# Turning v for a channel-attention kernel: eight TensorE transposes per group, or block loads and one VectorE transpose

## The chip, the cores and the metric

The kernel runs on one core of a Trainium2 chip. The metric is the device time of one execution in microseconds (us). The engines are called by the names that the profile uses: PE is TensorE (matmul; PEld is its weight load), DVE is VectorE, ACT is ScalarE, POOL is GpSimd, and SP is the engine that issues the DMAs here.

## What is computed

For each of four batches, q, k and v are 6080 tokens by 256 channels, all float32. Channel attention is followed by a feed-forward layer with a rational activation:

```
qn = q / (norm(q, axis=tokens) + 1e-6);  kn likewise
a  = softmax(kn.T @ qn / tau)            # 256 x 256, per batch
x  = v @ a                               # tokens x 256
h  = x @ w_in                            # 256 -> 2048
P  = a0 + a1 h + a2 h^2 + a3 h^3
Q  = 1 + |b0| |h| + |b1| h^2
out = (P / (Q + 1e-6)) @ w_out           # 2048 -> 256
```

## The kernel before

The attention matrix of a batch is folded into w_in once per batch (`fuse`), so that the main work on the tokens is h = v @ (a @ w_in), the activation, and the product with w_out. The tokens of a batch are cut into 12 groups, 11 of 512 tokens (four rows of 128) and one of 448; over four batches that is 48 groups. The 2048 hidden units are cut into eight pairs of 128, so a group has eight calls of `pair`. Each pair computes h in two PSUM banks (`mm1`, 12 matmuls of 512 columns: high and low parts of the weights and of v, the low times low product left out), runs the activation in about ten steps on ACT, DVE and POOL, and accumulates the product with w_out in PSUM (`mm2`, two halves, each with its own step). `finish` copies the group's result out and stores it.

The matmul `mm1` wants v with channels on the partitions. `values` makes that: it loads the group's v with tokens on the partitions (tile `vst`, one buffer), turns it with eight PE transposes of 128x128 into a PSUM buffer of the kind `hx`, and splits it there into a high part `vhi` (ACT, a copy that rounds) and a low part `vlo` (DVE, the difference). There are two buffers each of `vhi` and `vlo`, three of `hx` (which the pairs use for h) and one accumulator `acc`; together they fill PSUM.

The order of the instructions on each engine is not the order of the program text. Every step is handed to a `Planner` with an engine, a cost, a due time ("key") and the buffers that it reads and writes. The planner plays the engines forward in time: an engine that is free takes the ready step with the lowest key whose buffers are free. What it writes out is the order on each engine, and nothing else; costs, keys and latencies have no other effect on the chip. Buffers of the kinds in its `fifo` list are given out in the order of the keys. The due times come from the tables `LAG` (steps of a pair) and `TIME` (all else). Steps marked as using the port (all of POOL's, and DVE's steps that read and write only SBUF) are played one after the other between DVE and POOL.

Batch 0's scores are computed before the first group; 12 halves of batch 1's keys and queries are also read and multiplied early (`FRONT`); the rest of the next batch's attention is mixed into the groups. Each half of a group's q and k is loaded by two DMAs, squared on ACT and summed on POOL (some of batch 0's on DVE). The weights w_in and w_out arrive as 64-bit floats and are converted on DVE; four pieces of w_out are converted late, in the tiles `cv` and `cv2`.

Of the kernel before, what the change touches and what calls it, by code (L numbers as in the profile page):

```python
# [18 lines left out]


LAG = {
    "first": 2.42, "prod": 2.04, "abs": -4.64, "line": 9.56, "second": 3.75, "sum": -23.6, "slope": 5.71,
    "num1": 23.17, "num2": 21.53, "root": 8.83, "one": -1.7, "square": -3.23, "again": 5.54, "quot": 8.31,
    "last": 10.3, "out": 23.21,
}
TIME = {
    "pair": 3.57, "start": 48.71, "load": 1.9, "softmax": 48.77, "in": 5, "late_in": 3.83, "out0": 2.3,
    "out": 5.39, "attn0_0": -0.02, "attn_0": 0.98, "attn0": 3.82, "attn": 2.42, "attn1": 91.81, "value": 3.3,
    "fuse": 1.77, "finish": 10.12, "front": 45.32, "front_pace": 2.4,
}  # L30


# [35 lines left out]
class Planner:  # L68
# [42 lines left out]
    def order(self):  # L111
# [10 lines left out]
        busy["SP"] = 3.0  # L122
        events, out, now = [(3.0, 2, 0, None)], [], 0.0
        port = {"DVE": 0.0, "POOL": 0.0}
        for s in self.steps:
            if not s.need:
                heapq.heappush(ready[s.eng], (s.key, s.n, s))
# [12 lines left out]
        while left:  # L140
            for e in ready:
                while busy[e] <= now and ready[e]:
                    skipped, pick = [], None
                    while ready[e]:
                        entry = heapq.heappop(ready[e])
                        if fits(entry[2]):
                            pick = entry[2]
                            break
                        skipped.append(entry)
                    for entry in skipped:  # L150
                        heapq.heappush(ready[e], entry)
# [15 lines left out]
                    heapq.heappush(events, (busy[e], 0, pick.n, pick))  # L167
                    heapq.heappush(events, (busy[e] + self.HOP[e], 1, pick.n, pick))
            if not left:
                break  # L170
            assert events, [(e, h[0][0], [b.tag for b in h[0][2].new], dict(free)) for e, h in ready.items() if h]
            now = events[0][0]
            while events and events[0][0] <= now:
                _, what, _, s = heapq.heappop(events)
                if what == 2:
                    continue
                for t in s.after:
                    if (what == 0) == (t.eng == s.eng and s.eng != "SP"):
# [13 lines left out]
def tile_channel_attention_rational_ffn(  # L192
# [15 lines left out]
    P = 128  # L208
# [387 lines left out]


    def pair(m, at, vparts, w, acc):
# [20 lines left out]
                        )  # L619
                    idx += 1  # L620

        step("PE", 2.8 * s, at, mm1, [whi, wlo, vhi, vlo], [hx])

        if m >= NFP and p in FACTORED:
            fn = lambda: act.activation(c(kk), c(hx), AF.Abs, scale=b1)
            step("ACT", 1.12 * s, at + LAG["first"], fn, [hx], [kk])
            fn = lambda: dve.scalar_tensor_tensor(c(d), c(kk), b0, c(hx), op0=ALU.add, op1=ALU.mult)
            step("DVE", 1.28 * s, at + LAG["prod"], fn, [kk, hx], [d])
            fn = lambda: act.activation(c(d), c(d), AF.Abs)
            step("ACT", 1.02 * s, at + LAG["abs"], fn, [d], [d])  # L630
        else:
            fn = lambda: act.activation(c(d), c(hx), AF.Square)
            step("ACT", 1.02 * s, at + LAG["first"], fn, [hx], [d])
            fn = lambda: pool.tensor_scalar(c(d), c(d), b1, ONE, op0=ALU.mult, op1=ALU.add)
            step("POOL", 1.13 * s, at + LAG["line"], fn, [d], [d])
            fn = lambda: act.activation(c(kk), c(hx), AF.Abs, scale=b0)
            step("ACT", 1.12 * s, at + LAG["second"], fn, [hx], [kk])
            fn = lambda: pool.tensor_tensor(c(d), c(d), c(kk), op=ALU.add)
            step("POOL", 2.38 * s, at + LAG["sum"], fn, [d, kk], [d])

        fn = lambda: act.activation(c(y), c(hx), AF.Identity, scale=a3, bias=a2)
        step("ACT", 1.2 * s, at + LAG["slope"], fn, [hx], [y])
        fn = lambda: dve.tensor_tensor(c(y), c(y), c(hx), op=ALU.mult)
        step("DVE", 1.22 * s, at + LAG["num1"], fn, [y, hx], [y])
        fn = lambda: dve.scalar_tensor_tensor(c(hx), c(y), a1, c(hx), op0=ALU.add, op1=ALU.mult)
        step("DVE", 1.28 * s, at + LAG["num2"], fn, [y, hx], [hx])
# [3 lines left out]
        step("ACT", 1.06 * s, at + LAG["root"], fn, [d], [r])  # L650
        if m >= NFP and p in FACTORED:
            fn = lambda: pool.tensor_scalar(c(d), c(d), ones[:, 0:1], ONE, op0=ALU.mult, op1=ALU.add)
            step("POOL", 1.13 * s, at + LAG["one"], fn, [d], [d])
        fn = lambda: act.activation(c(r), c(r), AF.Square)
        step("ACT", 1.06 * s, at + LAG["square"], fn, [r], [r])
        fn = lambda: pool.tensor_tensor(c(d), c(d), c(r), op=ALU.mult)
        step("POOL", 2.38 * s, at + LAG["again"], fn, [d, r], [d])
        fn = lambda: dve.scalar_tensor_tensor(c(hx), c(hx), a0, c(r), op0=ALU.add, op1=ALU.mult)
        step("DVE", 1.28 * s, at + LAG["quot"], fn, [hx, r], [hx])
# [3 lines left out]
        step("DVE", 1.28 * s, at + LAG["last"], fn, [d, hx], [g])  # L663

        def mm2(i):
            for t in range(T):
# [5 lines left out]

        for i in range(2):
            old = [] if p == 0 and i == 0 else [acc]
            step("PE", 1.72, at + LAG["out"] + 0.1 * i, lambda i=i: mm2(i), [g, w_out_ok[p], *old], [acc])

    def finish(G, at, acc):
        b, g = divmod(G, NG)
        base, pn = groups[g]
        orow = buf("orow", [P, T, C])  # L680
        step("ACT", 1.05, at, lambda: act.copy(orow[:pn], acc[:pn]), [acc], [orow])
# [64 lines left out]
```

## Time and profile before

| what | value |
|---|---|
| time, median of 3 runs | 2692.95 us (2692.72 to 2694.38) |
| span of the profiled execution | 2694.6 us, 32473 instructions |
| PE busy | 2653.3 us, 98% |
| DVE, ACT, POOL busy | 2247.6, 2195.5, 2106.4 us (83%, 81%, 78%) |
| granted TensorE clock, mean | 0.995 |

The span runs from the first to the last instruction of the program with its last DMA; no other time is listed for the profiled execution. A busy time is the share of the span in which an engine had an instruction in flight. The ends of matmuls are modelled, so the start of one matmul to the start of the next tells more than their durations.

### The profile page before, as it was taken

The page shows a single profiled execution, that of the slowest core. Times are in us where ns is not written, and L with a number is a line of the kernel's source. Part 1 is how long each engine was busy: PE and PEld are TensorE (multiplying, and loading weights), DVE is VectorE, ACT ScalarE, POOL GpSimd, SP SyncE. Part 2 cuts the span into 40 slices and gives each one's busy share as a digit, 9 for nine tenths or more (in the row PEclk, how much of TensorE's full clock was granted, in tenths as well). Part 3 has the DMA queues.
Part 4 walks back from the last instruction along what each step waited for, and adds up shares of the span by engine and source line. Part 5 has one row for each costly group of instructions (what it writes and reads, how often), then busy time and mean ns, then how long its engine had stood idle before and what let it go on. Part 6 is the DMA issues. An engine that isn't in the chain of part 4 may idle for free.

```text
span 2694.6 us, 32473 instructions
## 1 busy us (share of the span) xinstructions
PE 2653.3 (98%) x12200; PEld 2271.6 (84%) x12200; DVE 2247.6 (83%) x1987; ACT 2195.5 (81%) x2227; POOL 2106.4 (78%) x1104
## 2 busy tenths in 40 slices
PE   7999999999999999999999999999999999999999
PEld 6778888888888888888888888888888888888887
DVE  7988888888878778788888878788888888888886
ACT  5778888888788888788878888877887888888885
POOL 6789877877678788877868888877875787787785
PEclk9999999999999999999999999999999999999999
DMA  9402000000011111100001111100000000000000
GB/s 325 134 32 80 28 16 32 16 18 30 16 31 47 55 55 48 45 32 31 17 16 31 55 55 48 47 30 32 15 16 16 31 16 16 32 16 17 31 9 15
DMA packets 69325, 110.10 MB, mean 41 GB/s; under 512 B 5296, under 2 KB 53936, under 8 KB 69168
## 3 DMA queue, kind: packets, MB, share of 16 engines
q1 hardware_dynamic: 69168, 108.03, 12.3%
q8 instruction: 96, 1.57, 0.2%
q14 instruction: 61, 0.50, 0.1%
HBM read 83.10 MB, written 24.90 MB: 40 GB/s over the span
## 4 chain that ended last, share of the span: by engine, by line
PE 90%; DVE 3%; POOL 1%; issue 1%; ACT 1%; DVEq 0%; POOLq 0%
PE acc L43 47%; PE hx L43 44%; DVE hx L43 1%; POOL d L43 1%; DVE g L43 1%; DVE sq L43 0%; ACT r L43 0%; DVE cv L43 0%; DVE uu L43 0%; DVE y L43 0%; DVE n L43 0%; DVE vlo L43 0%; DVE e L43 0%; ACT d L43 0%; DVE sm L43 0%
## 5 line engine op out<-in xcount | busy, mean ns | idle before, releaser
L43 PE MATMUL acc<-w_out_sb,g 128*128 128x256 f32 (+1 forms) x6144 | 1371.1, 379 | 0.0
L43 PEld LDWEIGHTS acc<-w_out_sb,g 128*128 128x128 f32 (+1 forms) x6144 | 1157.0, 189 | 167.6
L43 POOL TENSOR_TENSOR d<-d,r 128x1024 f32<-128x1024 f32 (+1 forms) x384 | 906.2, 2362 | 187.1 <-ACT r L43 172.9
L43 PE MATMUL hx<-vhi,w 128*128 128x512 f32 (+1 forms) x3072 | 892.5, 401 | 10.4 <-DVE g L43 5.5
L43 PEld LDWEIGHTS hx<-vhi,w 128*128 128x128 f32 x3072 | 579.1, 189 | 125.5 <-ACT sq L43 10.3
L43 DVE TENSOR_TENSOR uu<-uu,hx 128x1024 f32<-128x1024 f32 (+1 forms) x384 | 462.4, 1204 | 189.0 <-ACT uu L43 187.9
L43 POOL TENSOR_TENSOR d<-d,uu 128x1024 f32<-128x1024 f32 (+1 forms) x243 | 573.9, 2362 | 20.3
L43 DVE SCALAR_TENSOR_TENSOR hx<-hx,coef,r 128x1024 f32<-128x1024 f32 (+1 forms) x384 | 490.3, 1279 | 118.1 <-ACT r L43 101.2
L43 DVE SCALAR_TENSOR_TENSOR g<-d,hx 128x1024 f32<-128x1024 f32 (+1 forms) x384 | 463.5, 1207 | 47.2 <-POOL d L43 11.1
L43 DVE SCALAR_TENSOR_TENSOR hx<-uu,coef,hx 128x1024 f32<-128x1024 f32 (+1 forms) x384 | 489.6, 1275 | 7.8
L43 PE MATMUL hx<-vlo,w 128*128 128x512 f32 (+1 forms) x1536 | 474.3, 390 | 0.0
L43 ACT ACTIVATE uu<-hx,coef 128x1024 f32<-128x1024 f32 (+1 forms) x384 | 458.6, 1194 | 0.0
L43 ACT ACTIVATE uu<-hx,babs 128x1024 f32<-128x1024 f32 (+1 forms) x384 | 424.4, 1105 | 26.6 <-PE hx L43 26.6
L43 ACT ACTIVATE r<-d 128x1024 f32<-128x1024 f32 (+1 forms) x384 | 404.1, 1052 | 50.8 <-POOL d L43 46.4
L43 ACT ACTIVATE d<-hx 128x1024 f32<-128x1024 f32 (+1 forms) x243 | 247.0, 1017 | 226.3 <-PE hx L43 226.1
L43 ACT ACTIVATE r<-r 128x1024 f32<-128x1024 f32 (+1 forms) x384 | 403.2, 1050 | 12.1
L43 POOL TENSOR_SCALAR d<-d,babs 128x1024 f32<-128x1024 f32 (+1 forms) x243 | 272.8, 1123 | 166.9 <-ACT d L43 165.8
L43 PEld LDWEIGHTS hx<-vlo,w 128*128 128x128 f32 x1536 | 289.4, 188 | 58.6
L43 POOL TENSOR_SCALAR d<-d,ones 128x1024 f32<-128x1024 f32 (+1 forms) x141 | 157.5, 1117 | 140.9 <-ACT r L43 140.8
L43 ACT ACTIVATE d<-d 128x1024 f32<-128x1024 f32 (+1 forms) x141 | 146.4, 1038 | 57.4 <-DVE d L43 57.4
L43 POOL TENSOR_TENSOR ssq<-sq,ssq 128x1024 f32<-128x1024 f32 (+1 forms) x69 | 165.8, 2403 | 34.8 <-ACT sq L43 33.8
L43 DVE SCALAR_TENSOR_TENSOR d<-uu,babs,hx 128x1024 f32<-128x1024 f32 (+1 forms) x141 | 178.1, 1263 | 13.6 <-ACT uu L43 13.6
(83 smaller groups left out, 1087.3 us busy)
## 6 DMA issues: line engine op xcount, KB each, us to landing
vst<-in_v_dram SPq DMA_DIRECT2D x44, 512.0 KB, 3.5
out_dram<-orow SPq DMA_DIRECT2D x44, 512.0 KB, 2.6
kq<-in_k_dram SPq DMA_DIRECT2D x78, 256.0 KB, 3.7
kq<-in_q_dram SPq DMA_DIRECT2D x78, 256.0 KB, 4.0
d<-in_moe_w_in_dram SPq DMA_DIRECT2D x8, 512.0 KB, 7.0
r<-in_k_dram SPq DMA_DIRECT2D x10, 256.0 KB, 6.6
r<-in_q_dram SPq DMA_DIRECT2D x10, 256.0 KB, 6.6
d<-in_moe_w_out_dram SPq DMA_DIRECT2D x4, 512.0 KB, 7.0
```

The costliest lines, as they stand in the source:

```text
L43: ins = op(*args, **kwargs)
```

## The change

v is loaded straight in 32x32 blocks: eight DMAs per group, each to 32 partitions, in pieces of 32 floats (128 bytes). One DVE transpose of the whole group turns the blocks and writes `vT` into SBUF, in the buffer kind `cv`. ACT makes the high part from there, and the low part is made on POOL instead of DVE. The order of the tokens inside a group changes with it, so the store of the result writes rows of 256 floats (1 KB) instead of four rows in a piece. `LAG` now has a due time for each of the eight pairs, "in" is new, `TIME` has new numbers, the planner's costs are changed, and its single latency per engine becomes a table by producer and consumer.

```diff
-        vst = buf("vst", [P, T, C], F32)
-        slot = buf("hx", [P, 2, GT], F32, "vT")
+        vst, vT = buf("vst", [P, NC2, GT // 32, 32]), buf("cv", [P, NC2, GT], F32, "vT")
         hi, lo = buf("vhi", [P, NC2, GT], F32R), buf("vlo", [P, NC2, GT], F32R)
-        fn = lambda: sp.dma_start(vst[:pn], v[b, base : base + pn * T].rearrange("(p t) c -> p t c", t=T))
-        step("SP", 1.5, at - 3 * II, fn, gate, [vst])
-        def turned():
-            for c in range(NC2):
-                for t in range(T):
-                    pe.transpose(
-                        slot[:, c, t * pn : (t + 1) * pn], vst[:pn, t, c * P : (c + 1) * P], ident[:pn, :pn]
-                    )
-        step("PE", 1.1, at, turned, [vst], [slot, hi, lo])
-        step("ACT", 1.05, at + 1, lambda: act.activation(hi[:, :, :n], slot[:, :, :n], AF.Copy), [slot], [hi])
-        fn = lambda: dve.tensor_tensor(
-            lo[:, :, :n], slot[:, :, :n], hi[:, :, :n].bitcast(F32), op=ALU.subtract
-        )
-        step("DVE", 1.2, at + 2, fn, [slot, hi], [lo])
+        def load():
+            src = v[b, base : base + n].rearrange("(i t) (e j c) -> j e t i c", t=32, e=NC2, c=32)
+            for j in range(4):
+                for e in range(NC2):
+                    sp.dma_start(vst[32 * j : 32 * j + 32, e, : n // 32], src[j, e])
+        step("SP", 1.5, at - TIME["ahead"], load, gate, [vst])
+        whole = "p e i c -> p e (i c)"
+        fn = lambda: dve.transpose(vT[:, :, :n], vst[:, :, : n // 32].rearrange(whole))
+        step("DVE", 1.13, at, fn, [vst], [vT, hi, lo], True)
+        step("ACT", 0.95, at + TIME["vhi"], lambda: act.activation(hi[:, :, :n], vT[:, :, :n], AF.Copy), [vT], [hi])
+        fn = lambda: pool.tensor_tensor(lo[:, :, :n], vT[:, :, :n], hi[:, :, :n].bitcast(F32), op=ALU.subtract)
+        step("POOL", 2.36, at + TIME["vlo"], fn, [vT, hi], [lo], True)
...
-        step("PE", 2.8 * s, at, mm1, [whi, wlo, vhi, vlo], [hx])
+        step("PE", 2.73 * s, at + LAG["in"][p], mm1, [whi, wlo, vhi, vlo], [hx])
...
-        fn = lambda: sp.dma_start(out[row : row + pn * T].rearrange("(p t) e -> p t e", t=T), orow[:pn])
+        fn = lambda: sp.dma_start(out[row : row + pn * T].rearrange("(t p) e -> p t e", t=T), orow[:pn])
...
-    "pair": 3.57, "start": 48.71, "load": 1.9, "softmax": 48.77, "in": 5, "late_in": 3.83, "out0": 2.3,
+    "pair": 3.595, "start": 60.906, "load": 1.647, "softmax": 51.889, "in": 4.172, "late_in": 1.942,
...
-    "fuse": 1.77, "finish": 10.12, "front": 45.32, "front_pace": 2.4,
+    "attn1": 90.81, "value": 29.778, "fuse": 1.861, "finish": 25.52, "front": 40.417,
+    "front_pace": 1.878, "ahead": 14.939, "vhi": 23.877, "vlo": 28.867,
...
-    HOP = {"PE": 0.25, "ACT": 0.07, "DVE": 0.07, "POOL": 0.07, "SP": 3.5}
+    HOP = {"PE": 0.25, "ACT": 0.13, "DVE": 0.12, "POOL": 0.07, "SP": 3.5}
```

## Rows read from the trace of the kernel before

**Rows 1.** Busy time of each engine by stretch: us, then engine busy (instructions), clock, DMA.
```profile
0.00:80.00 80.00, 62.91 (x259) 51.48 (x260) 61.69 (x91) 42.21 (x50) 44.04 (x26) 0.96 0.92 294
80.00:180.00 100.00, 90.82 (x388) 76.02 (x388) 91.31 (x88) 78.03 (x90) 92.53 (x44) 0.93 0.24 74
180.00:200.00 20.00, 19.80 (x94) 16.75 (x93) 17.23 (x15) 14.84 (x16) 13.37 (x8) 1.00 0.32 106
200.00:300.00 100.00, 100.00 (x464) 85.88 (x463) 81.47 (x69) 83.06 (x83) 89.29 (x46) 1.00 0.20 62
300.00:600.00 300.00, 300.00 (x1379) 256.86 (x1378) 260.43 (x216) 255.66 (x251) 238.18 (x126) 1.00 0.06 22
600.00:2640.00 2040.00, 2031.62 (x9401) 1744.11 (x9400) 1706.01 (x1485) 1693.85 (x1714) 1601.50 (x842) 1.00 0.10 31
```

**Rows 2.** Busy time of each engine, columns as before, over one late group.
```profile
2498.80:2549.20 50.40, 50.40 (x234) 43.15 (x232) 43.62 (x37) 43.08 (x43) 39.79 (x22) 1.00 0.06 22
```

**Rows 3.** Waits of PE: what it waited for, us in total, times, longest.
```profile
PE hx L43 <- DVE sm L43: 8.4, 3, 2.8
```

**Rows 4.** Timeline of PE: start, us to the last end, matmuls merged.
```profile
2545.74 3.62 PE L43 MATMUL acc<-w_out_sb,g 128*128 128x256 f32 x16
2549.20 1.04 PE L43 MATMUL hx<-ident,vst 128*128 128x128 f32 x8
2550.07 1.89 PE L43 MATMUL acc<-w_out_sb,g 128*128 128x256 f32 x8
...
2599.59 0.93 PE L43 MATMUL hx<-ident,vst 112*128 112x112 f32 x8
2600.35 1.91 PE L43 MATMUL acc<-w_out_sb,g 128*128 128x256 f32 x8
```

**Rows 5.** Instructions on tile vst: count, duration min/median/max, first and last start.
```profile
L43 PE MATMUL hx<-ident,vst x384: 257/273/332, 52.0 to 2600.3; 128*128 128x128 f32 x176, 112*128 112x112 f32 x16
```

**Rows 6.** Groups by shape: count, busy us, mean ns, idle before.
```profile
L43 POOL TENSOR_TENSOR d<-d,r 128x1024 f32<-128x1024 f32 x352 | 838.6, 2385 | 145.1 <-ACT r L43 132.9 <-POOL ssq L43 0.9 <-POOL d L43 0.3
L43 DVE TENSOR_TENSOR vlo<-hx,vhi 128x1024 fp32r<-128x1024 f32 x44 | 53.6, 1218 | 2.6 <-ACT vhi L43 2.5
L43 ACT ACTIVATE vhi<-hx 128x1024 fp32r<-128x1024 f32 x44 | 44.8, 1018 | 7.3 <-PE hx L43 7.2
L43 ACT ACTIVATE sq<-kq 128x1024 f32<-128x1024 f32 x74 | 77.5, 1054 | 13.8 <-POOL orow L43 8.9 <-POOL ssq L43 3.0 <-DMA kq<-in_q_dram 1.6
L43 DVE TENSOR_TENSOR orow<-sq,orow 128x1024 f32<-128x1024 f32 x5 | 6.1, 1223 | 1.8 <-POOL orow L43 1.8
```

**Rows 7.** DVE on tile cv (SBUF only): duration min/median/max, ns.
```profile
L43 DVE TENSOR_TENSOR cv<-cv,cv x4: 680/1838/2733, 66.5 to 144.0; 128x512 f32<-128x512 f32 x4
```

**Rows 8.** DMA of the span: queue, packets, share; issues, KB each, us to landing.
```profile
q1 hardware_dynamic: 69168, 108.03, 12.3%
vst<-in_v_dram SPq DMA_DIRECT2D x44, 512.0 KB, 3.5
out_dram<-orow SPq DMA_DIRECT2D x44, 512.0 KB, 2.6
kq<-in_k_dram SPq DMA_DIRECT2D x78, 256.0 KB, 3.7
```

**Rows 9.** Timeline of SP in the first stage: start, us, DMA issued.
```profile
18.31 0.37 SPq L43 DMA_DIRECT2D r<-in_k_dram  x1
19.02 0.37 SPq L43 DMA_DIRECT2D r<-in_q_dram  x1
```

**Rows 10.** The chain that ended last, its end: start, us, what.
```profile
2667.00 22.46 PE acc L43 x104
2689.46 0.02 issue
2689.49 1.01 ACT orow L43
```

More of the change, by code (lines that the diff above doesn't have):

```diff
@@ L68 @@
 class Planner:
-    HOP = {"PE": 0.25, "ACT": 0.07, "DVE": 0.07, "POOL": 0.07, "SP": 3.5}
+    HOP = {"PE": 0.25, "ACT": 0.13, "DVE": 0.12, "POOL": 0.07, "SP": 3.5}
+    LAT = {
+        "PE": {"PE": 0.0, "ACT": 0.27, "DVE": 0.27, "POOL": 0.3, "SP": 3.5},
+        "ACT": {"PE": 0.16, "ACT": 0.23, "DVE": 0.14, "POOL": 0.2, "SP": 3.5},
+        "DVE": {"PE": 0.14, "ACT": 0.13, "DVE": 0.23, "POOL": 0.24, "SP": 3.5},
+        "POOL": {"PE": 0.11, "ACT": 0.07, "DVE": 0.07, "POOL": 0.11, "SP": 3.5},
+        "SP": {"PE": 3.5, "ACT": 3.5, "DVE": 3.5, "POOL": 3.5, "SP": 3.5},
+    }
     def __init__(self, slots, fifo, banks):
@@ L124, in order @@
         port = {"DVE": 0.0, "POOL": 0.0}
+        engines = list(self.HOP)
         for s in self.steps:
@@ L166, in order @@
                         b.owner, b.until = e, busy[e] + self.HOP[e]
-                    heapq.heappush(events, (busy[e], 0, pick.n, pick))
+                    heapq.heappush(events, (busy[e], 0, pick.n, None))
                     heapq.heappush(events, (busy[e] + self.HOP[e], 1, pick.n, pick))
+                    for c, lat in enumerate(self.LAT[e].values()):
+                        heapq.heappush(events, (busy[e] + lat, 10 + c, pick.n, pick))
             if not left:
@@ L174, in order @@
                 _, what, _, s = heapq.heappop(events)
-                if what == 2:
+                if s is None:
                     continue
                 for t in s.after:
-                    if (what == 0) == (t.eng == s.eng and s.eng != "SP"):
+                    if what >= 10 and t.eng == engines[what - 10]:
                         t.need -= 1
@@ L620, in mm1 @@
                     idx += 1
-        step("PE", 2.8 * s, at, mm1, [whi, wlo, vhi, vlo], [hx])
+        step("PE", 2.73 * s, at + LAG["in"][p], mm1, [whi, wlo, vhi, vlo], [hx])
         if m >= NFP and p in FACTORED:
             fn = lambda: act.activation(c(kk), c(hx), AF.Abs, scale=b1)
-            step("ACT", 1.12 * s, at + LAG["first"], fn, [hx], [kk])
+            step("ACT", 1.0 * s, at + LAG["first"][p], fn, [hx], [kk])
             fn = lambda: dve.scalar_tensor_tensor(c(d), c(kk), b0, c(hx), op0=ALU.add, op1=ALU.mult)
-            step("DVE", 1.28 * s, at + LAG["prod"], fn, [kk, hx], [d])
+            step("DVE", 1.2 * s, at + LAG["prod"][p], fn, [kk, hx], [d])
@@ L629, in pair @@
             fn = lambda: act.activation(c(d), c(d), AF.Abs)
-            step("ACT", 1.02 * s, at + LAG["abs"], fn, [d], [d])
+            step("ACT", 0.94 * s, at + LAG["abs"][p], fn, [d], [d])
         else:
             fn = lambda: act.activation(c(d), c(hx), AF.Square)
-            step("ACT", 1.02 * s, at + LAG["first"], fn, [hx], [d])
+            step("ACT", 0.94 * s, at + LAG["first"][p], fn, [hx], [d])
             fn = lambda: pool.tensor_scalar(c(d), c(d), b1, ONE, op0=ALU.mult, op1=ALU.add)
-            step("POOL", 1.13 * s, at + LAG["line"], fn, [d], [d])
+            step("POOL", 1.1 * s, at + LAG["line"][p], fn, [d], [d])
@@ L636, in pair @@
             fn = lambda: act.activation(c(kk), c(hx), AF.Abs, scale=b0)
-            step("ACT", 1.12 * s, at + LAG["second"], fn, [hx], [kk])
+            step("ACT", 1.0 * s, at + LAG["second"][p], fn, [hx], [kk])
             fn = lambda: pool.tensor_tensor(c(d), c(d), c(kk), op=ALU.add)
-            step("POOL", 2.38 * s, at + LAG["sum"], fn, [d, kk], [d])
+            step("POOL", 2.36 * s, at + LAG["sum"][p], fn, [d, kk], [d])
         fn = lambda: act.activation(c(y), c(hx), AF.Identity, scale=a3, bias=a2)
-        step("ACT", 1.2 * s, at + LAG["slope"], fn, [hx], [y])
+        step("ACT", 1.09 * s, at + LAG["slope"][p], fn, [hx], [y])
@@ L649, in pair @@
         fn = lambda: act.activation(c(r), c(d), AF.Abs_reciprocal_sqrt, bias=more)
-        step("ACT", 1.06 * s, at + LAG["root"], fn, [d], [r])
+        step("ACT", 0.97 * s, at + LAG["root"][p], fn, [d], [r])
         if m >= NFP and p in FACTORED:
             fn = lambda: pool.tensor_scalar(c(d), c(d), ones[:, 0:1], ONE, op0=ALU.mult, op1=ALU.add)
-            step("POOL", 1.13 * s, at + LAG["one"], fn, [d], [d])
+            step("POOL", 1.1 * s, at + LAG["one"][p], fn, [d], [d])
         fn = lambda: act.activation(c(r), c(r), AF.Square)
-        step("ACT", 1.06 * s, at + LAG["square"], fn, [r], [r])
+        step("ACT", 0.97 * s, at + LAG["square"][p], fn, [r], [r])
@@ L656, in pair @@
         fn = lambda: pool.tensor_tensor(c(d), c(d), c(r), op=ALU.mult)
-        step("POOL", 2.38 * s, at + LAG["again"], fn, [d, r], [d])
+        step("POOL", 2.36 * s, at + LAG["again"][p], fn, [d, r], [d])
         fn = lambda: dve.scalar_tensor_tensor(c(hx), c(hx), a0, c(r), op0=ALU.add, op1=ALU.mult)
-        step("DVE", 1.28 * s, at + LAG["quot"], fn, [hx, r], [hx])
+        step("DVE", 1.2 * s, at + LAG["quot"][p], fn, [hx, r], [hx])
         fn = lambda: dve.scalar_tensor_tensor(
@@ L662, in pair @@
         )
-        step("DVE", 1.28 * s, at + LAG["last"], fn, [d, hx], [g])
+        step("DVE", 1.2 * s, at + LAG["last"][p], fn, [d, hx], [g])
         def mm2(i):
@@ L674, in pair @@
             old = [] if p == 0 and i == 0 else [acc]
-            step("PE", 1.72, at + LAG["out"] + 0.1 * i, lambda i=i: mm2(i), [g, w_out_ok[p], *old], [acc])
+            step("PE", 1.727, at + LAG["out"][p] + 0.1 * i, lambda i=i: mm2(i), [g, w_out_ok[p], *old], [acc])
     def finish(G, at, acc):
@@ L680, in finish @@
         orow = buf("orow", [P, T, C])
-        step("ACT", 1.05, at, lambda: act.copy(orow[:pn], acc[:pn]), [acc], [orow])
+        step("ACT", 0.92, at, lambda: act.copy(orow[:pn], acc[:pn]), [acc], [orow])
         row = b * N + base
-        fn = lambda: sp.dma_start(out[row : row + pn * T].rearrange("(p t) e -> p t e", t=T), orow[:pn])
+        fn = lambda: sp.dma_start(out[row : row + pn * T].rearrange("(t p) e -> p t e", t=T), orow[:pn])
         step("SP", 1.5, at + 2, fn, [orow], [Buf()])
```

26 lines of the change are left out of this document (20 added, 6 removed).

## The prediction

> **What bounds the kernel now.** I read the busy times by stretch first [rows 1]. From 200 to 600 us PE is busy for every one of the 400 us, and from 600 to 2640 for 2031.6 of 2040; the 8.4 missing there are three waits for the softmax of batches 1 to 3 [rows 3]. The reader should see that this is one long stretch with one limit, while DVE, ACT and POOL stand between 78% and 89%. Since busy PE need not be PE at its pace, I looked at one late group by itself [rows 2]: 50.40 us, all of it PE's, with 43.62 us of DVE, 43.08 of ACT and 39.79 of POOL. The timeline of PE [rows 4] confirms it by starts: 16 matmuls take 3.46 us from 2545.74 to 2549.20, 0.216 each, and the next block begins on that beat. So PE issues without a pause, and what leaves its stream shortens the stretch.
>
> The first 200 us are different. Up to 80 us the DMA engines are 92% busy at 294 GB/s and PE idles for 17.1 us. From 80 to 180 us POOL is busy for 92.5 us and DVE for 91.3, PE for 90.8 [rows 1]: here the first groups, which use POOL most, and the late weight pieces compete, and PE waits for them. In 0 to 200 us PE idles for 26.5 us in all (17.1 + 9.2 + 0.2). The end is PE's again: 22.46 us of products with w_out, 104 matmuls or 13 half steps, which ran behind, then 1.01 us of copy and the last store, from about 2690.5 to 2694.6 [rows 10].
>
> **The change, part by part.** *PE.* Eight transposes per group go. Their cost is from their start to that of the next block: 2549.20 to 2550.07, so 0.87 us; for a group of 448 tokens 2599.59 to 2600.35, so 0.76 us [rows 4]. There are 44 and 4 such blocks 384 transposes in all [rows 5]: 44 x 0.87 + 4 x 0.76 = 41.3 us. The three blocks before 200 us lie where PE is not the limit, so I take 3 x 0.87 = 2.6 us of that back: 38.7 us. Nothing else of PE's work changes.
>
> *DVE.* It loses the low part, 1.218 us per group [rows 6], and gains the transpose, which the trace doesn't show. The lower bound is half of the row for 1024 elements of SBUF, 1.223 us [rows 6], so 0.6; the upper is the same row with POOL in the way: a 512-element step on SBUF tiles took from 0.680 to 2.733 us in the stage where POOL is busiest [rows 7], 2.05 us more, so 3.3. I take 1.2, the row with one DVE pass over as many elements. Even at 3.3 a group has 43.62 - 1.22 + 3.3 = 45.7 us of DVE in 49.5. The cover is the 13 half steps by which the products with w_out run behind; without it each step queued behind the transpose would pass 2.05 us on to PE, 98 us over the run. ACT's high part reads SBUF instead of PSUM: 1.054 against 1.018 us for such rows [rows 6], 1.7 us in all 48 groups, against some 6 us of ACT's slack in each.
>
> *POOL.* It gains the low part, 2.385 us as its other two-source steps [rows 6], and perhaps waits for the transpose (0 to 1.2). A group then has 42.2 to 43.4 us of POOL in 49.5. In its fullest stretch after the start, 200 to 300 us, POOL goes from 89.3 to 94.1 with two low parts per 100 us, at most 96.5. That leaves it under PE, so the steady groups pay nothing. Between 80 and 180 us POOL is itself the limit: two low parts (groups 1 and 2) are 4.8 us there, its idle time is 7.5, and I charge half, 2.4 (bounds 0 and 4.8).
>
> *The load.* One DMA of 128 partitions becomes eight with 4096 pieces of 128 bytes, 256 for each of 16 engines. No row shows such a piece. Below: by bytes, 512 KB at the 294 GB/s of the first stage [rows 1], 1.8 us. Above: the mean packet of the span, 12.3% of 16 x 2694.6 us over 69168 packets [rows 8], is 76.7 ns, so 19.6 us. Near: 1 KB pieces, of which q and k consist, at 294 GB/s take 56 ns, so 14.3 us, plus about 2 for what the 3.5 us landing [rows 8] has beyond its bytes: 16 us. I take that. In a steady group it is hidden: `vst` is free once the transpose has read it, and its next contents are wanted a group later, 49.5 us. The eight issues, at 0.71 us from one to the next as in the first stage [rows 9], take 5.7 us of SP; behind them on SP stand the store of the group before and loads of q and k, which have two buffers or more. At the start the load of group 0 falls at key 51.889 - 14.939 = 36.95, ahead of the last of batch 0's 24 halves (23 x 1.647 = 37.88). It can hold that half back by 0 to 18 us (19.6 less the 1.8 that 512 KB took anyway). I charge 0, because the 12 halves of batch 1 that are multiplied early give PE something to do, and price the other end as a rival.
>
> The Trainium skill ("DMA: Bandwidth & Descriptors", Specifications) says that transfers reach line rate from 512 bytes on, and that below it the engines read, modify and write. If that doubled the 56 ns, a load would take 29 us, still inside a group's 49.5, and the sum would stand; no row here shows a piece that small.
>
> *The rest.* `vT` no longer takes one of three `hx` buffers, so the pairs wait less for PSUM; PE had no such waits to lose in the steady stretch, so 0. `vT` shares `cv` with the late w_out pieces; group 1's has the key 60.9 + 29.778 x 3.595 = 168, behind the last of them (60.9 + 30.0 + 5.793 x 7 = 131), and may hold group 1 back: that is inside the 4.8. The store in 1 KB rows: 512 KB land in 2.6 us now and 256 KB in 1 KB rows in 3.7 [rows 8], so the last store takes 0 to 1.1 us longer, 0.5. The due times, costs and latencies move every step. In the steady stretch there is nothing to gain but the 8.4 us of softmax waits; at the start there are 26.5 us of PE's idle time to gain, and as much work could be put in the wrong place. I take 0 and keep both ends.
>
> **Sum.** 2694.6 - 38.7 + 2.4 + 0.5 = 2658.8 us of span. The median of the runs is 1.65 us below the profiled span, so 2657.
>
> **The rivals.** *The start is held by the small pieces* (chance 0.12). For it: DMA is 92% busy there, and softmax, fusing and the first pair follow one upon the other. Against: one half in 24 is behind. Price 10 to 18 us: 2667 to 2675, to 2682 with the other 2.4 of POOL and a few more.
>
> *The start is better planned* (0.09). The 26.5 us of idle are the room. If 12 to 27 are won: 2645 down to 2630.
>
> *The freed time is refilled* (0.05). PE may be at its pace only because the other engines just keep up; if DVE, at 45.7 us plus what it waits for, can't do a group in under 50.4, PE gets gaps and the time stays at 2693. Against: in 200 to 300 us PE ran full with POOL at 89.3, and DVE has 4.7 us less than that per group even at the upper end.
>
> *The low part comes late* (0.07, the other side). A group's first product needs `vlo`. It now waits for three steps on three engines, the last on POOL behind two-source steps of 2.385 us. If it is late by one such step in every group, that is 48 x 2.385 = 114 us: 2771. It decides against the change from 36 / 48 = 0.75 us per group. For it: POOL is the engine that gains work, and its due time puts the step behind almost everything. Against: two buffers allow it to be made nearly a group ahead.
>
> *The load outlasts the group* (0.03). A q or k load has 16 pieces for each engine and lands in 3.7 us [rows 8], 231 ns per piece with all latency in it. At that price 256 take 59.1 us; with 1.2 us of transpose the groups follow at 60.3. They come every (2600.3 - 52.0) / 47 = 54.2 us now [rows 5], 53.4 without the transposes, so 47 x 6.9 = 324 us more: 2981. It decides from (53.4 - 1.2) x 1000 / 256 = 204 ns per piece, against 56. The Trainium skill ("VectorE: DVE Perf Modes", The three transpose paths) speaks against this change: a plain DMA that transposes by strides is 19 times slower than the hardware's own. Taken on the 3.5 us landing it would be 66.5 us, and the run about 3330 us; but the innermost run here stays 128 bytes long, and no run has shown it yet.
>
> **How the numbers follow.** The likeliest case, PE still the limit and the start about as long, has 0.64 and its own range 2645 to 2668: 2.4 or 4.8 us of POOL, 8.4 us of softmax and part of the idle time at the start. The range for the whole, 2640 to 2682, takes in the start held by small pieces and half of the better-planned start, and leaves out 0.05 + 0.05 + 0.07 + 0.03 = 0.20. What a measurement can tell from no change is 0.2%, 5.4 us. Faster by more than that: 0.64 + 0.12 + 0.09 = 0.85. Same: 0.05. Slower: 0.07 + 0.03 = 0.10.
>
> **What would show it.** After the change PE should again be busy without a gap from 200 us on, a late group should last about 49.5 us instead of 50.40, and the transposes' rows should be gone. POOL should have 48 steps more of about 2.4 us and some 84% of the span, DVE 48 transposes of 1.2 us (over 2 shows POOL in the way). A load of v should land in some 16 us; over 50 would be the last rival. PE waiting for POOL's `vlo`, or for ACT or DVE in the steady stretch, would make the forecast wrong, and so would a stretch before 200 us that holds more idle time of PE than now.

## The result, and the profile after

The changed kernel takes 2670.02 us (median of 4 runs, 2665.86 to 2672.19), the kernel before 2692.84 us on the same chip (4 runs, 2691.62 to 2694.38): a ratio of 0.9912, 95% interval 0.9898 to 0.9926. That is 22.8 us faster where 36 were forecast, inside the range of 2640 to 2682 and 2 us above the likeliest case's own range.

The page of the changed kernel, the profiled execution (its time is 2665.86 us, 1.76 above its span):

```profile
span 2664.1 us, 32250 instructions
...
PE 2615.4 (98%) x11816; PEld 2233.5 (84%) x11816; DVE 2220.9 (83%) x1987; ACT 2169.9 (81%) x2227; POOL 2219.6 (83%) x1152
...
DMA packets 281423, 110.11 MB, mean 41 GB/s; under 512 B 205232, under 2 KB 278192, under 8 KB 281264
...
q1 hardware_dynamic: 281264, 108.05, 15.8%
```

Busy time by stretch, columns and stretches as in [rows 1]; then two late groups, from the copy of one result to that of the next but one (late copies come 50.4 and 48.7 us apart in turn), and the two stretches that end with the copy of group 0's and of group 46's result:

```profile
0.00:80.00 80.00, 61.66 (x244) 50.43 (x245) 58.39 (x88) 43.83 (x48) 52.61 (x29) 0.94 0.99 316
80.00:180.00 100.00, 85.07 (x358) 69.83 (x357) 85.16 (x89) 73.03 (x86) 85.18 (x41) 0.95 0.25 62
180.00:200.00 20.00, 19.80 (x90) 16.59 (x90) 18.07 (x16) 17.86 (x19) 17.67 (x10) 1.00 0.08 26
200.00:300.00 100.00, 100.00 (x455) 85.84 (x454) 79.60 (x68) 81.30 (x81) 89.54 (x46) 1.00 0.22 57
300.00:600.00 300.00, 300.00 (x1358) 256.25 (x1357) 259.90 (x218) 254.26 (x252) 257.40 (x134) 1.00 0.12 29
600.00:2640.00 2040.00, 2030.11 (x9233) 1739.50 (x9232) 1713.35 (x1507) 1694.10 (x1739) 1712.02 (x893) 1.00 0.13 31
...
2425.30:2524.40 99.10, 99.10 (x450) 84.65 (x449) 86.24 (x73) 84.87 (x85) 84.26 (x44) 1.00 0.10 21
...
0.00:185.30 185.30, 152.03 (x625) 124.88 (x626) 147.99 (x179) 122.16 (x139) 143.08 (x72) 0.94 0.56 170
...
185.30:2621.40 2436.10, 2426.01 (x11018) 2077.31 (x11017) 2052.08 (x1790) 2027.49 (x2067) 2056.40 (x1070) 1.00 0.13 32
```

The same two stretches of the kernel before, up to the same two copies:

```profile
0.00:178.60 178.60, 152.33 (x640) 126.36 (x640) 151.71 (x177) 118.84 (x138) 135.17 (x68) 0.94 0.55 173
...
178.60:2655.40 2476.80, 2468.21 (x11410) 2118.18 (x11408) 2078.42 (x1794) 2060.68 (x2074) 1956.33 (x1029) 1.00 0.10 32
```

The reader should see three parts of the difference. From the copy of group 0 to that of group 46 the changed kernel takes 2436.1 us in place of 2476.8, 40.7 less, and PE is as full as before: 10.1 us idle in place of 8.6. Up to group 0's copy it takes 185.3 us in place of 178.6, 6.7 more, and PE idles for 33.3 us in place of 26.3. What follows group 46's copy takes 42.7 us in place of 39.2, 3.5 more, of which 37.3 in place of 32.8 are PE's work: less of the last group's work had been done by then. Together: -40.7 + 6.7 + 3.5 = -30.5, the difference of the two spans.

The groups of the parts of the change, by shape, as in [rows 6]:

```profile
L58 POOL TENSOR_TENSOR d<-d,r 128x1024 f32<-128x1024 f32 x352 | 838.2, 2384 | 165.9 <-ACT r L58 155.9 <-issue 2.6
L58 POOL TENSOR_TENSOR vlo<-cv,vhi 128x1024 fp32r<-128x1024 f32 x44 | 105.2, 2391 | 7.2 <-ACT vhi L58 6.2
L58 DVE STREAM_TRANSPOSE cv<-vst 128x1024 f32<-128x1024 f32 x44 | 54.3, 1235 | 1.0 <-DMA vst<-in_v_dram 1.0
L58 ACT ACTIVATE vhi<-cv 128x1024 fp32r<-128x1024 f32 x44 | 47.0, 1067 | 2.8 <-DVE cv L58 2.8
```

The transpose takes 1235 ns and waits for a load for 1.0 us in all. The DMA issues, as in [rows 8], and the instructions on tile `vst`, as in [rows 5]:

```profile
vst<-in_v_dram SPq DMA_DIRECT2D x352, 64.0 KB, 2.3
out_dram<-orow SPq DMA_DIRECT2D x44, 512.0 KB, 2.9
kq<-in_k_dram SPq DMA_DIRECT2D x78, 256.0 KB, 4.0
```

```profile
L58 SPq DMA_DIRECT2D vst<-in_v_dram x384: 311/486/3867, 46.3 to 2499.2; - x192
L58 DVE STREAM_TRANSPOSE cv<-vst x48: 1101/1234/1245, 56.9 to 2545.4; 128x1024 f32<-128x1024 f32 x44, 128x896 f32<-128x896 f32 x4
```

Each of the eight DMAs lands in 2.3 us, and the issues follow at some 0.49 us, so a load of v is there about 8 x 0.486 + 2.3 = 6.2 us after its first issue, not 16. PE's waits from 200 us to 2640, which answer to [rows 3], and the end of the chain, which answers to [rows 10]:

```profile
PE hx L58 <- DVE g L58: 9.9, 4, 3.3
```

```profile
2639.73 19.01 PE acc L58 x88
2658.74 0.02 issue
2658.76 1.01 ACT orow L58
```

Three of the four waits, 3.2 to 3.3 us each, come at the change of a batch, as the three of [rows 3] did. The end is PE's as before, with 88 matmuls or 11 half steps instead of 13. At the start, the first products of group 0 and the scores of batch 0's softmax, in the instructions on tiles `vhi` and `sq` (count, duration, first and last start), first before, then after:

```profile
L43 PE MATMUL hx<-vhi,w x22: 387/390/763, 86.0 to 109.5; 128*128 128x512 f32 x22
L43 DVE SCALAR_TENSOR_TENSOR sq<-hx,n,y x2: 475/480/485, 73.9 to 74.3; 128x256 f32<-128x256 f32 x2
```

```profile
L58 PE MATMUL hx<-vhi,w x16: 387/390/579, 97.4 to 106.3; 128*128 128x512 f32 x16
L58 DVE SCALAR_TENSOR_TENSOR sq<-hx,n,y x2: 468/470/471, 83.4 to 83.8; 128x256 f32<-128x256 f32 x2
```

The scores come 9.5 us later and the first product 11.4 us later. The theory to test is: the gain is PE's transposes, 0.87 us a group, and the loss at the start comes from the new due times. The rivals: the small pieces of v hold the start; the gain comes from the due times and not from the path; the steady groups have another limit just under the new pace.

### The profile page after: what moved, and what is told of

Its sections match the earlier page's. It is cut to its first block, busy times and chain, and to the rows that moved or that the text cites. A ratio compares the mean times of both kernels' runs of the same rounds, so it can differ in the third digit from the quotient of the medians.

```text
span 2664.1 us, 32250 instructions
## 1 busy us (share of the span) xinstructions
PE 2615.4 (98%) x11816; PEld 2233.5 (84%) x11816; DVE 2220.9 (83%) x1987; ACT 2169.9 (81%) x2227; POOL 2219.6 (83%) x1152
## 2 busy tenths in 40 slices
DMA packets 281423, 110.11 MB, mean 41 GB/s; under 512 B 205232, under 2 KB 278192, under 8 KB 281264
## 3 DMA queue, kind: packets, MB, share of 16 engines
q1 hardware_dynamic: 281264, 108.05, 15.8%
## 4 chain that ended last, share of the span: by engine, by line
PE 93%; DVE 3%; DMA 2%; ACT 1%; issue 1%; SPq 0%; POOL 0%; POOLq 0%; ACTq 0%
PE acc L58 48%; PE hx L58 44%; DMA kq<-in_q_dram 1%; DMA r<-in_k_dram 1%; DVE e L58 0%; DMA kq<-in_k_dram 0%; DVE g L58 0%; SPq L58 0%; DVE hx L58 0%; DVE uu L58 0%; ACT uu L58 0%; ACT r L58 0%; DMA r<-in_q_dram 0%; DVE sq L58 0%; DMA g<-in_moe_w_out_dram 0%
## 5 line engine op out<-in xcount | busy, mean ns | idle before, releaser
L58 PE MATMUL hx<-vhi,w 128*128 128x512 f32 (+1 forms) x3072 | 916.5, 405 | 9.2 <-DVE g L58 9.2
L58 DVE SCALAR_TENSOR_TENSOR d<-uu,babs,hx 128x1024 f32<-128x1024 f32 (+1 forms) x141 | 178.3, 1264 | 42.7 <-ACT uu L58 42.5
```

The lines of the kernel that those rows point to most:

```text
L58: ins = op(*args, **kwargs)
```

## The experiments

Times are medians; the kernel before, run beside them, took 2692.8 to 2693.0 us. In the diffs a minus is the changed kernel. The planner writes each kernel's order anew from its due times. In the runs with PE's time back, with v in large pieces, with the transpose done twice and with less of PE, the traces show every instruction that stays in the changed kernel's order, on PE, DVE, ACT and POOL alike; in all other runs the order differs.

**The old path in the new order.** `values` and the store are those of the kernel before, with all the new tables; only the due times inside `values` (the turn at 3.3 pairs, the load, the high and the low part) are the old ones.

```diff
-            vparts.append(values(G + 1, at + TIME["value"] * II, gate if G == 0 else ()))
+            vparts.append(values(G + 1, at + 3.3 * II, gate if G == 0 else ()))
```

> The load, the eight PE transposes, the low part on DVE and the store are those of the kernel before; due times, costs and latencies of the planner are the new ones (the turn of v has its old due times). Theory (PE's 41.3 us of transposes are the steady gain, and the new order costs some 8 us at the start): 2692.8 plus 0 to 8, so 2693 to 2701, with PE busy without a gap from 200 us on and 50.4 us a group. Rival (the gain comes from the new due times): 2660 to 2680.

Measured: 2728.71 us (2728.17 to 2729.16), ratio 1.0135 (1.0119 to 1.0150).

```profile
PE hx L58 <- DVE g L58: 15.0, 21, 3.3
PE hx L58 <- DVE sm L58: 10.3, 3, 3.4
...
PE acc L58 <- ACT orow L58: 4.4, 12, 0.6
```

Both the theory and the rival missed. With the new due times the old path is 36 us slower than with the old ones, so the due times alone are no gain. PE idles 32.5 us in the first 200 us, where the kernel before idled 26.5, and 22.6 us from there to 2640 us, where it idled 8.4. That is 20 of the 36 us; the rest is open. That the turn takes one of three `hx` buffers would fit the waits for `g` (18 of the 21 come after 200 us, 7.9 us in all), but no run tested it. The first product comes at 98.7 us here, as late as in the changed kernel (97.4), with the old loads.

**The new path in the old order.** The kernel before with the new `values` and the new store, and the old due times for its steps.

```diff
-        step("SP", 1.5, at - TIME["ahead"], load, gate, [vst])
+        step("SP", 1.5, at - 3 * II, load, gate, [vst])
...
-        step("ACT", 0.95, at + TIME["vhi"], lambda: act.activation(hi[:, :, :n], vT[:, :, :n], AF.Copy), [vT], [hi])
+        step("ACT", 0.95, at + 1, lambda: act.activation(hi[:, :, :n], vT[:, :, :n], AF.Copy), [vT], [hi])
...
-        step("POOL", 2.36, at + TIME["vlo"], fn, [vT, hi], [lo], True)
+        step("POOL", 2.36, at + 2, fn, [vT, hi], [lo], True)
```

> The block loads, the DVE transpose, the low part on GpSimd and the store in 1 KB rows, with due times, costs and latencies of the kernel before (its due times for the load, the turn, the high and the low part too). Theory: the steady stretch gains the same, so groups of 49.5 us; the start can be shorter or longer. 2652 to 2672. Rival (the old due times can't carry the new path, because GpSimd has more to do): PE has gaps in the steady stretch, groups over 50 us, 2680 or more.

Measured: 2715.46 us (2712.68 to 2718.47), ratio 1.0085 (1.0072 to 1.0099). Its stretch from 80 to 180 us and its waits of PE:

```profile
80.00:180.00 100.00, 74.66 (x305) 60.23 (x304) 80.43 (x80) 65.27 (x78) 82.02 (x38) 0.90 0.27 74
```

```profile
PE hx L43 <- DVE g L43: 41.7, 24, 9.3
```

The rival held in its time and in PE's gaps: without new due times the path loses 22.6 us, and PE idles in the first groups and waits for DVE's `g`. That GpSimd's work makes these gaps is not shown. The first product comes at 87.3 us, about as in the kernel before. With the run above this is a square: the first product is at 86 to 87 us with the old due times and at 97 to 99 with the new ones, whichever path is in it. PE's idle time in the first 200 us is 26.5 us (old path) and 43.3 (new path) with the old due times, 32.5 and 33.5 with the new ones. So the later first product belongs to the due times, and the old path too pays some 6 us for them at the start, without small pieces.

**PE's time back.** Four matmuls of 512 columns more in the first pair of each group, into a bank that the next matmul overwrites.

```diff
+            for i in range(4 if p == 0 else 0):
+                pe.matmul(hx[:, 0, :n], whi[:, 0, 0:P], vhi[:, 0, :n], start=True, stop=True)
```

> The changed kernel, and in the first pair of each group four more matmuls of 512 columns into the bank that the real product then overwrites: 4 x 0.216 = 0.86 us of PE per group, as much as the transposes had taken; nothing else moves. Theory (PE time is the whole gain in the steady stretch): 48 x 0.86 = 41 us more, 2706 to 2713. Rival (the gain comes from the freed PSUM buffer, or from DVE, and PE has room): under 2690.

Measured: 2713.83 us (2708.50 to 2714.89), 43.8 us over the changed kernel, with PE as full as there:

```profile
600.00:2640.00 2040.00, 2030.09 (x9200) 1736.47 (x9200) 1685.10 (x1478) 1663.10 (x1704) 1684.23 (x876) 1.00 0.13 31
```

192 matmuls for 43.8 us are 0.228 us each, not 0.216, which puts the time 0.8 us over the theory's range. What PE is given back counts in full: PE is the limit of the changed kernel, in an order that is otherwise the same. The freed `hx` buffer is still free here, so it is not what makes the steady gain.

**v in large pieces**, for group 0 alone and then for all groups: one DMA with 4 KB rows; the transpose stays, but what it turns is not v in its blocks, so that these kernels compute something else.

```diff
+            if G in BIG:
+                flat = vst[:pn].rearrange("p e i c -> p (e i c)")
+                sp.dma_start(flat, v[b, base : base + n].rearrange("(p t) c -> p (t c)", t=T))
+                return
```

> The changed kernel, but the v of group 0 alone is loaded by one DMA in 4 KB rows, so that group 0's v is not turned rightly; all orders are the same. Theory (the small pieces of the first load, 8.8 us of SP's issuing at 46 to 55 us, hold up the loads behind them and with them part of the start): 4 to 8 us less, 2662 to 2666. Rival (the start is longer because the due times put weight pieces and early products ahead of the first scores): 2668 to 2672, as the changed kernel.

> The changed kernel with every group's v loaded by one DMA in 4 KB rows (so v is not turned rightly in any group); all orders are the same. Theory (the small pieces are hidden in the steady stretch, and group 0's cost nothing either, as its own run with large pieces showed): 2666 to 2672. Rival (the 4096 pieces and eight issues per group cost something each group, or make the runs of the changed kernel spread over 6 us where those of before spread over 3): 2655 to 2664, or runs within 2 us.

Measured: group 0 alone 2669.78 us (2665.43 to 2670.47), all groups 2668.27 us (2665.23 to 2670.70), against 2670.02. Neither differs from the changed kernel by 0.2%. The first row below is the load of group 0 in the first kernel, the other two are of the second:

```profile
vst<-in_v_dram SPq DMA_DIRECT2D x1, 512.0 KB, 10.3
```

```profile
q1 hardware_dynamic: 87408, 108.03, 12.8%
...
vst<-in_v_dram SPq DMA_DIRECT2D x44, 512.0 KB, 3.6
```

At the start even the large piece takes 10.3 us; in the first 80 us the DMA engines of the changed kernel are 99% busy. The small pieces cost nothing that the time shows: they raise the DMA engines' share of the span from 12.8% to 15.8%.

**The low part on DVE**, at the same due time.

```diff
-        fn = lambda: pool.tensor_tensor(lo[:, :, :n], vT[:, :, :n], hi[:, :, :n].bitcast(F32), op=ALU.subtract)
-        step("POOL", 2.36, at + TIME["vlo"], fn, [vT, hi], [lo], True)
+        fn = lambda: dve.tensor_tensor(lo[:, :, :n], vT[:, :, :n], hi[:, :, :n].bitcast(F32), op=ALU.subtract)
+        step("DVE", 1.14, at + TIME["vlo"], fn, [vT, hi], [lo], True)
```

> The changed kernel with the low part of v back on DVE (1.2 us instead of 2.4 on GpSimd), same due time. Theory (the steady stretch is PE's whichever engine makes the low part; DVE would have 44.9 us of 49.5 a group): steady groups of 49.5 us and 2664 to 2674. Rival (GpSimd's new work is what costs the start its 8 us): 2660 to 2664. Other rival (DVE has no room for it): over 2680.

Measured: 2741.90 us (2735.23 to 2743.82), 71.9 over the changed kernel.

```profile
L58 DVE TENSOR_TENSOR vlo<-cv,vhi x48: 1084/1920/3208, 59.2 to 2626.3; 128x1024 fp32r<-128x1024 f32 x44, 128x896 fp32r<-128x896 f32 x4
```

```profile
PE hx L58 <- DVE g L58: 47.3, 33, 10.5
PE acc L58 <- ACT orow L58: 12.8, 15, 2.1
```

The step with two sources in SBUF takes from 1.084 to 3.208 us on DVE, while the transpose, with one source, stays between 1.103 and 1.245 in the same kernel. The theory missed, and the time lies where the rival "DVE has no room" put it. But the run changes more than the engine of the low part: the planner wrote another order, in which 5496 of PE's 11816 matmuls stand in other places than in the changed kernel. So it shows that the low part costs less on POOL with these due times, and not by which cause.

**The transpose done twice**, the second over the first; no other instruction moves.

```diff
-        fn = lambda: dve.transpose(vT[:, :, :n], vst[:, :, : n // 32].rearrange(whole))
+        def fn():
+            dve.transpose(vT[:, :, :n], vst[:, :, : n // 32].rearrange(whole))
+            return dve.transpose(vT[:, :, :n], vst[:, :, : n // 32].rearrange(whole))
```

> The changed kernel with VectorE's transpose of each group done twice, the second one writing the same values over the first; the order of all other instructions stays. It adds 1.23 us of VectorE to each of 48 groups, some 59 us in all, without a step that stands beside GpSimd's. The prediction left the transpose's cost off the path as long as VectorE has room in a group. Theory: it does, 42.5 + 1.23 = 43.7 us of 49.5, so the time stays within some 6 us of the changed kernel, 2665 to 2676, and what made the low part on VectorE cost 72 us was its place and its stretched duration, not the amount of VectorE's work. Rival: in this order each step queued behind on VectorE passes its delay on to TensorE, and the time rises by up to 59 us, 2700 to 2729.

Measured: 2677.04 us (2674.26 to 2679.44), 7.0 over the changed kernel and 1 us over the bound given.

```profile
L58 DVE STREAM_TRANSPOSE cv<-vst x96: 1106/1244/1249, 57.5 to 2558.0; 128x1024 f32<-128x1024 f32 x88, 128x896 f32<-128x896 f32 x8
```

Of 59 us of DVE's work 52 are hidden, in an unchanged order. DVE has the room that the prediction counted on for this much work. The low part of the run above was more, 87.7 us in 48 steps, but its 71.9 us are ten times these 7.0; whether they come from the stretched step, from its place or from the other order, no run told apart.

**Less of PE.** Matmuls are left out of the first pair of each group. The expectation says six of twelve; the edit left out four (the low products of the second half of the channels), 0.91 us a group at 0.228 each, 43.8 us in all.

```diff
+                        if p == 0 and e == 1 and idx > 3:
+                            continue
```

> The changed kernel with six of the twelve matmuls of the first pair of each group left out (two high and four low products of the second half of the channels, so h of that pair is not complete): 6 x 0.228 = 1.37 us less PE per group, 66 us in all; orders are the same. Theory (PE is still the only limit after the change): 2604 to 2612. Rival (the change has brought the other engines within reach, GpSimd at 85% first): the gain is less than two thirds, 2626 or more, and PE shows gaps in the steady stretch.

Measured: 2632.72 us (2631.88 to 2633.83), 37.3 less than the changed kernel.

```profile
600.00:2600.00 2000.00, 1988.08 (x9015) 1699.22 (x9015) 1700.60 (x1495) 1683.13 (x1728) 1702.22 (x888) 1.00 0.13 32
```

```profile
PE hx L58 <- DVE g L58: 12.9, 13, 3.2
```

The stretch ends at 2600 us here, because the last matmul of this kernel ends at 2626.6. PE idles for 11.9 of its 2000 us, the changed kernel for 9.9 of the same. From 200 to 2600 us PE waits 13 times for `g`, 12.9 us in all; the changed kernel waits 4 times, 9.9 us. So PE is still the limit, and 85% of what it loses comes off the time, more than the rival's two thirds. Of the 6.5 us that are missing, 3.0 are these waits; the rest is within the 6 us by which runs of one kernel differ. Two late groups take 97.9 us in place of 99.1, 0.6 us less each and not 0.91, with one of nine new waits of 0.34 us in them.

**The start.** Four edits of due times there: batch 0's softmax 14 us sooner, with and without the folding into w_in that follows it; the four early pieces of w_out 12 us later; both.

```diff
-    attns = [Attn(0, 0.0, TIME["load"], TIME["softmax"])]
+    attns = [Attn(0, 0.0, TIME["load"], TIME["softmax"] - SOON)]
```

> The changed kernel with one due time moved: the softmax of batch 0 is due 14 units sooner (37.9 instead of 51.9), before the conversion of the four early pieces of w_out (41.4 to 53.9). Theory (in the new order DVE converts weight pieces for about 10 us between the norms and the first scores, so the first product of group 0 starts at 97.4 us instead of 86.0): first product before 90 us, 2658 to 2665. Rival (the first 200 us are bound by the sum of DVE's and GpSimd's work, not by when the scores come): 2667 to 2672.

```diff
+            own, at = at, at - (SOON if self.b == 0 else 0.0)
...
-            self.w = [self.fuse(p, at + 1 + TIME["fuse"] * p, eT, stat) for p in range(NFP)]
+            self.w = [self.fuse(p, own + 1 + TIME["fuse"] * p, eT, stat) for p in range(NFP)]
```

> The changed kernel with the softmax of batch 0 due 14 us sooner, as tried before, but with the steps that fold its matrix into w_in left at their own due times. Theory: when all of it was due sooner, the folding of the later pairs went ahead of the first products of group 0 and cost what the softmax had won. With the folding left in place the first product comes at 86 to 90 us and the time is 2658 to 2665. Rival: the start is bound by the sum of VectorE's and GpSimd's work by about 180 us, and the order of it is worth nothing: 2666 to 2673. A second rival is a worse order from there on, over 2675.

```diff
-        c = 8.0 + TIME["in"] * n
+        c = 8.0 + TIME["in"] * n + (12.0 if side == "out" else 0.0)
```

> The changed kernel with one edit: the four early pieces of w_out are due 12 us later (53 to 66 in place of 41 to 54), so that they stand behind the softmax of batch 0, which is due at 51.9, as they do in the kernel before (48 to 63 against 48.8). Theory: the loss of the first 200 us in the changed kernel (33.5 us of PE's idle time against 26.5 before) comes from that order. VectorE converts w_out from 72.8 to 83.4 us there and comes to the softmax's scores only at 83.38, against 73.91 before. Then the scores come at 73 to 75, the first product of group 0 at 86 to 90 in place of 97.4, and the time is 2658 to 2665, some 5 to 12 us under the changed kernel's 2670. Rival: VectorE and GpSimd have the same total of work to do by about 180 us, so the pieces stand in the way of the first activations or of the products with w_out instead, and the time stays at 2666 to 2673. A second rival is a worse order from there on, over 2675.

> Both edits of the two runs beside it: the softmax of batch 0 due 14 us sooner with the folding left in place, and the early pieces of w_out due 12 us later. If the order at the start is what costs, this should be no slower than the better of the two, 2656 to 2663; if the sum of VectorE's and GpSimd's work bounds the start, 2666 to 2673 again.

Measured, with the first product of group 0 and PE's idle time in the first 200 us:

| kernel | time, us | first product | idle |
|---|---|---|---|
| the changed kernel | 2670.02 | 97.4 | 33.5 |
| softmax sooner, folding too | 2679.24 (2678.68 to 2679.85) | 101.2 | 42.9 |
| softmax sooner, folding kept | 2782.67 (2775.99 to 2783.73) | 90.5 | 42.0 |
| pieces of w_out later | 2788.92 (2784.15 to 2792.76) | 104.4 | 44.5 |
| both | 2676.55 (2672.70 to 2680.47) | 91.8 | 36.0 |

None is faster, and the theory that the late scores cost the time fell: with both edits the first product comes 5.6 us sooner, PE idles 2.5 us more, and the granted clock from 80 to 180 us is 0.86 where the changed kernel has 0.95. Two of them lose 113 and 119 us, and not at the start. Here is the kernel with the folding kept, from 600 to 2640 us and around one wait, then PE's timeline there:

```profile
600.00:2640.00 2040.00, 1986.70 (x8915) 1687.85 (x8914) 1657.35 (x1454) 1625.63 (x1679) 1651.05 (x861) 0.99 0.13 31
...
1046.00:1052.00 6.00, 6.00 (x20) 4.88 (x21) 5.80 (x5) 5.36 (x6) 6.00 (x4) 0.72 0.00 0
1052.00:1060.00 8.00, 8.00 (x39) 6.89 (x38) 4.64 (x4) 5.66 (x6) 5.95 (x4) 1.00 0.20 68
```

```profile
1045.91 0.72 PE L58 MATMUL hx<-vhi,w 128*128 128x512 f32 x2 [2.07 <-DVE g L58]
1046.48 0.63 PE L58 MATMUL hx<-vlo,w 128*128 128x512 f32 x2
1046.95 1.67 PE L58 MATMUL hx<-vhi,w 128*128 128x512 f32 x4
...
1054.73 1.07 PE L58 MATMUL hx<-vhi,w 128*128 128x512 f32 x4
```

From the copy of group 38 to that of group 46 it takes 416.3 us, the changed kernel 394.3, so 2.75 us less per group. PE idles for 53.3 of 2040 us in place of 9.9, and after the wait shown the granted clock is lower: 0.72 from 1046 to 1052 us, a mean of the levels of 1.2 and 2.4 GHz; four matmuls take 1.67 us there and 1.07 later. The edits touch due times of the start alone, but the planner writes another order for the groups after it too. In the two slow kernels 6840 and 6712 of PE's 11816 matmuls stand in other places than in the changed kernel; with the folding sooner too it is 436, with both edits 124, and these two lose 9.2 and 6.5 us. So the large loss goes with the other order, and it is more than the start could win.

## Why the prediction was right, and where its size was off

**PE's transposes, the main term, came out as worked out.** Between the two copies lie 46 blocks, 42 x 0.87 + 4 x 0.76 = 39.6 us; that stretch is 40.7 us shorter, and PE stays full [rows 1]. That the two agree within 1.1 us is partly luck, for 4.5 us of PE's work (37.3 in place of 32.8) also moved behind the second copy, and PE's busy time over the whole span falls by 37.9 us, not 41.3. The groups show it by themselves: two late groups are full of PE in 99.10 us, 49.55 each, where [rows 2] had 50.40. The run with PE's time put back shows that PE's time is the cause and not only the size.

**The side costs.** DVE's transpose was taken as 1.2 us and takes 1.235; its upper end of 3.3, with POOL in the way, did not occur. The Trainium skill ("SBUF — State Buffer", SBUF: two separate sides) says that GpSimd and VectorE lock each other out only where VectorE has two SBUF inputs or runs in a mode that uses both ports; the rows of the low part on DVE (1.084 to 3.208 us) and of the transpose beside it (1.103 to 1.245) agree. POOL's low part takes 2.391 us (2.385 taken), and POOL has 83% of the span (84%), but 89.5 us of the stretch from 200 to 300 us, not 94.1. The load lands in about 6 us where 16 were taken: the step "1 KB pieces ... take 56 ns" was too dear for a piece of 128 bytes, and hidden in any case. The eight issues take SP some 3.9 us in a steady group, not 5.7. ACT's high part takes 1067 ns, the store 2.9 us against 2.6 in [rows 8].

**What was off is the rest of the sum**, 12.9 us between 2657.15 and 2670.02. The medians differ by 22.8 us where the transposes alone are 41.3, so all else costs 18.5 us, and the sum charged 2.6 + 2.4 + 0.5 = 5.5. The profiled executions show 5.3 us of the miss and not the other 7.6.

- 5.3 us lie between the spans, 2664.1 against 2658.8. The step was "due times ... I take 0", with both ends left open. PE idles 33.5 us in the first 200 us where [rows 1] had 26.5, 7.0 more, against 2.6 + 2.4 = 5.0 charged; in the steady stretch it idles 1.5 us more, at the end 1.1 less where 0.5 was charged. PE's busy time falls by 37.9 us in place of 41.3, and what its other matmuls took more is not explained. The time is where the rival "small pieces" at the start put it (2667 to 2675), but the two runs with large pieces refute that cause. The old path under the new due times idles 32.5 us in the first 200 us, so the loss there comes with the due times. POOL isn't it, as "POOL is itself the limit" had it: from 80 to 180 us it is busy for 85.2 us, and for 88.1 from 91.4 to 191.4, less than the 92.5 of [rows 1].
- 7.6 us lie in which executions were profiled. In the runs of the kernel before that stand beside the experiments the time is 1.75 to 1.87 us above the span. So the execution with the span of 2694.6 was a long one of its kernel, some 3.4 us above the median of 2692.95; the step "-1.65" only brought the sum back to that median. The profiled execution of the changed kernel, 2665.86, is the quickest of its four, 4.2 us below their median. A typical pair is 7.6 us closer than the traced one, and why is open.
- The changed kernel's runs spread over 6.3 us, but that is no mark of the change: the kernel before, in the nine runs that stand beside each set of experiments, spreads over 5.7 to 6.8 us, and the spread stays with large pieces for all groups (5.5 us). In the kernel before the granted clock goes with it: beside the run with less of PE it took 2690.37 us at 0.998 and 2697.20 at 0.995. The median of its clock is 0.996 there, while the changed kernel's four runs have 0.993 to 0.994. Two thousandths of 2665 us are 5.3 us, an estimate from rounded values, so the clock may hold much of the 7.6 us; no run tested it.

**The rivals.** The low part did not come late: no wait of PE names it. The load did not outlast the group. The Trainium skill ("VectorE: DVE Perf Modes", The three transpose paths) has a plain DMA that transposes by strides 19 times slower than the hardware's own when the innermost stride at the destination is large. Taken on the plain load's 3.5 us that is an estimate of 66.5 us; the load here takes some 6.2 us, but its innermost run is 128 bytes long, so the page's case was not tested. The freed time was not refilled, and even of the next 43.8 us that PE gives up 37.3 arrive. The start was not better planned but worse: 7.0 us more of PE's idle time.

**What the prediction did not see** is that path and due times belong together. The path gives 58.7 us with the new due times (2728.71 to 2670.02) and costs 22.6 us with the old ones (2692.84 to 2715.46). Charging the due times nothing came near only for the two together, and that was luck: no row of the prediction shows it. How much of either number is the path's and how much the order's that the planner happened to write is not shown; an edit of 14 or 12 us at the start moved the time by over 110. Which of the new due times costs the 7 us at the start is not settled either: four tries moved the first product by -6.9 to +7.0 us, and none lowered the idle time.

## What to carry to other kernels

Where one engine issues without a pause, price an edit by that engine's start-to-start times, and expect most of it as long as its new pace is above what the others need; here a group lost 0.85 us of the 0.87 worked out, but the whole run only 22.8 of 41.3. When a step changes its engine and its buffers, its due times have to change with it: either alone can lose what both together win. When a planner writes the order, compare the orders before a difference is put down to the step that was edited. And before a difference of two profiles is set against one of medians, ask whether the profiled executions are typical; the offset of time to span in other runs tells.

## What the runs showed of the hardware

A transpose of 1024 columns in 32x32 blocks of 4 bytes takes VectorE 1.235 us, about as long as its subtraction of as many elements in the kernel before (1.218), and with GpSimd busy for 83% of the span none of 48 took longer than 1.245. A VectorE step with two sources in SBUF took 1.084 to 3.208 us. Loads in 128-byte pieces cost little: 64 KB land in 2.3 us, and 193,856 packets more than with large pieces (281,264 against 87,408) raise the share of 16 DMA engines by 3 points. One pause of PE of 2.07 us was followed by a granted clock of 0.72 over 6 us. Not every pause is: after the changed kernel's three waits of some 3.2 us at the change of a batch, the stretches of 15 us around them have clocks of 0.89, 0.89 and 1.00.
